# The opening of a fused Fourier-filter and maxout kernel: filter rows spread through PSUM by TensorE, X staged by ScalarE, GpSimd's pairs doubled by DMA

## The chip, the cores and the metric

One core of a Trainium2 chip runs the kernel. The metric is the device time of one execution in microseconds; it is the median of three runs. A profile is one execution recorded by the hardware profiler: its span runs from the first instruction to the last. Engines are called PE (TensorE), PEld (its weight loads), DVE (VectorE), ACT (ScalarE), POOL (GpSimd) and SP (SyncE, which here only issues DMAs).

## What is computed

The first half filters a sequence in the frequency domain; the second is a layer with two linear maps, a maximum and a third map.

```python
batch, seq, dim = (8, 3072, 256)
X = np.fft.rfft(x, axis=1)
F = (filt_r + 1j * filt_i)[None, :, :]
y = np.fft.irfft(X * F, n=x.shape[1], axis=1)      # x2 = y.reshape(24576, 256)
h1 = x2 @ w1                                       # w1, w2: 256 x 1024
h2 = x2 @ w2
out = np.maximum(h1, h2) @ w_out                   # w_out: 1024 x 256
```

## The kernel before

The transform of 3072 points is split into stages that are matrix products with small tables of sines. For a batch: stage 1 multiplies x (96 rows, 32 columns of 256) by `C1`; a transpose brings it into `bt`; stage 2 (`s2`) multiplies by the table `U` and gives the spectrum X in PSUM (`px`); a product with the filter F on a vector engine gives `pq`; stage 3 (`s3` or `s3t`) multiplies `pq` by the tables `VP` and `VQ`; a second transpose (`t2` in the first batch) gives `zr`; stage 4 (`s4`) multiplies by `G1` and gives `y_`, the filtered rows. Then `moe_h` and `moe_o` compute max(h1, h2) @ w_out as relu(x2 (w1 - w2)) @ w_out + x2 (w2 @ w_out). Eight batches are pipelined: while `moe_h` and `moe_o` run on batch b in 64 steps of eight blocks, the stages of batch b + 1 and b + 2 run between them at steps given by hand in `plan`, `mid` and `group`. The order on each engine is the order of the program (`manual_schedule`).

**The opening** is what stands ahead of the first `moe_h`: nothing of the long pipeline can cover it, so the first batch takes a shorter way, transposing through TensorE and not through DRAM (`s1t`, `t1`, `s3t`, `t2`). It runs in these steps.

- GpSimd loads x of batch 0 in eight pieces (`load_x`, L89) and F in sixteen (`load_f`, L122: two halves `WP`, columns w 0 to 8 and 8 to 12, two groups g, real and imaginary, two row blocks). Only rows 0 to 32 of each group of 64 are loaded; the other 32 rows are a copy of them, made by `double_f`: half 1 by DMAs on SP (L130), half 0 by VectorE (L128). `fix_f` (L145) then puts one row right.
- `table_c` and `tables_u` (VectorE, then sines on ScalarE, `sines_u`) make `C1` and `U`; `table_v(h, q)` turns U into the products for `VP` (q = 0) and `VQ` (q = 1) for half h of the filter pairs in PSUM, and `put_v` has ScalarE copy them. `table_g` makes `G1`.
- The twelve w columns are six pairs v = 0 to 5. For each, `s2(0, v)` gives two PSUM tiles `px`, s = 0 and 1, of 128 x 512, and each is multiplied with 1024 columns of F (real and imaginary): `product` (L390) on VectorE straight from PSUM, or on GpSimd from a copy in SBUF that ScalarE makes (`stage_x`, L652). VectorE has seven of the twelve tiles and three quarters of another (`shared_product`), GpSimd four and the remaining quarter.
- `s3t(v)` multiplies each pair's `pq` by VP and VQ: one product of `W1` that nobody reads (L581, two for v = 1), then 32 products (L587) into two PSUM tiles, which ScalarE (for g = 1 of v = 4 and 5, VectorE) evicts into `zT` (L597, L595).
- `t2(0)` transposes the first block of zT (L608), `s4(0)` makes the first `y_` (L460), and `moe_h` begins (L482). `f1` (L330 to L338) starts stage 1 of batch 1 between them.

PSUM tiles come from two pools: `ps` has six slots, `pso` two. `s3t` uses `ps` for odd v, `pso` for even; `table_v` uses `ps` for h = 0, `pso` for h = 1. A tile keeps its slot until its last reader is done. `spin(n)` issues n unread products of W1.

Pairs are done in the order 1, 0, 2, 3, 4, 5, and both halves of `table_v` and `put_v` stand ahead of the first `s3t`.

Of the kernel before, what the change touches and what calls it, by code (L numbers as in the profile page):

```python
# [27 lines left out]
def kernel(  # L28
# [29 lines left out]
    G2 = const.tile([128, 48], BF16)  # L58
    W1 = const.tile([128, 512], BF16)
# [64 lines left out]
    def double_f(h, g, ri, engine):  # L124
        w0, w1 = WP[h]
        o_, i_ = F[64 * g + 32:64 * g + 64, ri, w0:w1], F[64 * g:64 * g + 32, ri, w0:w1]
        if engine is V:
            V.tensor_copy(o_, i_)  # L128
        else:
            nc.sync.dma_start(out=o_, in_=i_)  # L130
# [13 lines left out]
    def fix_f():  # L144
        V.tensor_copy(F[32:33, 0, 0, 0], FZ[32:33, 0])  # L145
# [10 lines left out]

    hv = init.tile([128, 2, 1], FP32)
# [17 lines left out]
    for ri in range(2):  # L175
        put_fz(ri)
    load_f(0)
    load_f(1)

    def table_c():  # L180
# [10 lines left out]
        S.activation(C1, uc.rearrange("p k r -> p (k r)"), AF.Sin, bias=zero[0:NP], scale=TWO_PI)  # L191

# [58 lines left out]
    def table_g():  # L251
        pg = ps.tile([96, NP], FP32, tag="ps", name="pg")
        TE.matmul(pg, C1, I128[0:NP, 0:NP], start=True, stop=True)
# [68 lines left out]

    def f1(b, c, engine):
        if c == 0:
# [3 lines left out]
        at = at_[b]  # L328
        pa = ps.tile([96, 2, D], FP32, tag="ps", name="pa")
        TE.matmul(pa, C1, xb[b, c // 2][:, 2 * (c % 2):2 * (c % 2) + 2], start=True, stop=True)  # L330
# [9 lines left out]
    def f1_read(b):  # L340
        bt[b] = bpool.tile([128, NU, D], BF16, tag="bt", name="bt")
        src = ad[b].rearrange("(u q) m d -> (q m) u d", q=4)
        for u0, u1 in ((0, 4), (4, 12), (12, NU)):
            nc.sync.dma_start(out=bt[b][:, u0:u1], in_=src[:, u0:u1])
# [49 lines left out]
    def shared_product(v, s, px, xs_, pool):  # L394
        pq = pool.tile([128, 2, 2, D], BF16, tag="pq", name="pq")
        V.tensor_tensor(pq[:, 0], px, F[:, 0, 2 * v:2 * v + 2, s], OP.mult)
        V.tensor_tensor(pq[:, 1, 0], px[:, 0], F[:, 1, 2 * v, s], OP.mult)
        G.tensor_tensor(pq[:, 1, 1], xs_[:, 1], F[:, 1, 2 * v + 1, s], OP.mult)
        return pq
# [177 lines left out]
    def s3t(v, pq):  # L577
        pool, tag = (ps, "ps") if v % 2 else (pso, "po")
        pz = [pool.tile([128, 2, 2, 2, 2, NM], FP32, tag=tag, name="pt%d" % g) for g in range(2)]
        for _ in range(2 if v == 1 else 1):  # L580
            TE.matmul(pz[0].rearrange("p i s r c m -> p (i s r c m)"), W1[:, 0:128], W1, start=True, stop=True)  # L581
        for i in range(2):
            for s in range(2):
                for dc in range(2):
                    for q, tab in enumerate((VP, VQ)):
                        for g in range(2):
                            TE.matmul(pz[g][:, i, s, :, dc], pq[s][64 * g:64 * g + 64, q, i, 128 * dc:128 * dc + 128],  # L587
                                      tab[64 * g:64 * g + 64, 2 * v + i, s].rearrange("p (r m) -> p r m", r=2),
                                      start=(q == 0), stop=(q == 1))
        zv = zT.rearrange("p c m (w g) q -> p w g (c m) q", g=2)  # L590
        for g in range(2):
            o_ = zv[:, 2 * v:2 * v + 2, g]
            i_ = pz[g].rearrange("p i s r c m -> p i (c m) (s r)")
            if v >= 4 and g == 1:
                V.tensor_copy(o_, i_)  # L595
            else:
                S.activation(o_, i_, AF.Copy)  # L597

    def t2(c, engines):
# [3 lines left out]
        for k, engine in enumerate(engines):  # L603
            pr = ps.tile([96, n, D], BF16, tag="ps", name="pr")
            m0 = 4 * c + n * k
            for m in range(n):
                for dc in range(2):
                    TE.transpose(pr[:, m, 128 * dc:128 * dc + 128], zT[:, dc, m0 + m].rearrange("p u q -> p (u q)"),  # L608
# [14 lines left out]
    V.tensor_scalar(NI, cid, pid, -1.0, OP.is_equal, OP.mult)  # L623
    tables_u()
    for g in range(2):
        for ri in range(2):
            double_f(1, g, ri, nc.sync)
# [12 lines left out]
    zT = bpool.tile([128, 2, NM, NU, 4], BF16, tag="bt", name="zT")  # L640
    for n in range(6):
        t1(n, S if n % 2 else V)
    put_v(0, 0, table_v(0, 0))
    for g in range(2):
        for ri in range(2):
            double_f(0, g, ri, V)
    fix_f()
    xs = {}

    def stage_x(v):  # L650
        t_ = init.tile([128, 2, D], FP32, name="xs%d" % v)
        S.activation(t_, pxs[v][1], AF.Copy)  # L652
        xs[v] = t_

    POOLED = (0, 2, 3, 4)

    def products(v):
        pool = pq0 if v > 2 else pqpool
        pq = [product(V, v, 0, pxs[v][0], pool)]
        if v == 5:  # L660
            pq.append(shared_product(v, 1, pxs[v][1], xs[v], pool))
        else:
            pq.append(product(G, v, 1, xs[v], pool) if v in POOLED else product(V, v, 1, pxs[v][1], pool))
        return pq

    pqs = {}
    pxs = {v: s2(0, v) for v in (1, 0)}
    stage_x(0)
# [160 lines left out]
```

## Time and profile before

| What | Value |
|---|---|
| median of three runs | 497.84 us (497.64 to 498.34) |
| the profiled execution | 498.64 us, its span 496.8 us |
| PE busy over the span | 483.8 us (97%), 5759 products |
| DVE, ACT, POOL busy | 335.4 us (68%), 320.4 us (64%), 258.7 us (52%) |
| mean granted TensorE clock | 0.989 |
| last x piece used by `s1t` | 14.21 us |
| first product on VectorE (L390) | 23.76 us |
| first `s3t` (L581) | 25.97 us |
| `t2(0)` (L608) | 35.59 us |
| first `moe_h` product (L482) | 37.73 us |

The times in the last five rows are starts, in us from the start of the span. A busy TensorE is not TensorE at its peak, since its products are pipelined and their ends are modelled. The opening is the first 38 us, about 8% of the span; after it TensorE shows no gap longer than 1.3 us.

### The profile page before, as it was taken

How to read it: one execution, taken by the hardware profiler on the slowest of the kernel's cores; microseconds unless marked ns; L12 is line 12 of the kernel's file. 1: busy time of each engine (PE TensorE's matmuls, PEld its weight loads, DVE VectorE, ACT ScalarE, POOL GpSimd, SP SyncE). 2: the span in 40 equal slices, each digit the busy share in tenths (PEclk: the TensorE clock that was granted, in tenths of full speed). 3: DMA queues.
4: the chain of work that ended last, by engine and by line, in shares of the span. 5: the costliest groups of instructions: out<-in, count | busy, mean ns of one | idle time of the engine just before them, and what ended most of it. 6: DMA issues, size and time to landing. Idle time of an engine off the chain costs nothing.

```text
span 496.8 us, 14137 instructions
## 1 busy us (share of the span) xinstructions
PE 483.8 (97%) x5759; PEld 353.5 (71%) x5759; DVE 335.4 (68%) x535; ACT 320.4 (64%) x667; POOL 258.7 (52%) x342
## 2 busy tenths in 40 slices
PE   7699999999999999999999999999999999999997
PEld 3457777777777777777777777776777777777775
DVE  7886788468855688467855688457873688556542
ACT  5777478667775677576866668665766656464442
POOL 8694868318466594528646295536842212222220
PEclk9879999999999999999999999999999999999999
DMA  8989988996789867896789977897776834531112
GB/s 128 161 242 224 259 269 260 284 234 190 204 266 221 216 210 223 249 225 174 231 257 227 183 244 211 257 215 168 227 231 175 181 104 129 157 120 66 64 64 86
DMA packets 76626, 97.30 MB, mean 196 GB/s; under 512 B 7985, under 2 KB 54354, under 8 KB 75186
## 3 DMA queue, kind: packets, MB, share of 16 engines
q1 hardware_dynamic: 63218, 66.71, 52.1%
q0 software_dynamic: 13200, 29.60, 21.4%
q8 instruction: 45, 0.74, 0.7%
q14 instruction: 19, 0.16, 0.1%
q10 hardware_dynamic: 144, 0.09, 0.1%
HBM read 53.87 MB, written 47.19 MB: 203 GB/s over the span
## 4 chain that ended last, share of the span: by engine, by line
PE 92%; DMA 3%; ACT 2%; POOL 1%; issue 1%; DVE 0%; SPq 0%; POOLq 0%
PE po L536 34%; PE ph L482 33%; PE po L534 8%; PE pz L408 5%; PE pc L443 3%; PE px L384 2%; PE pa L355 2%; DMA xb<-in_x_dram 2%; DMA zr<-zd 1%; PE pt L587 1%; DMA zd<-zt 1%; PE pr L608 1%; POOL xb L89 1%; PE pt L581 1%; PE pa L330 1%
## 5 line engine op out<-in xcount | busy, mean ns | idle before, releaser
L486 ACT ACTIVATE gt<-ph 128x384 bf16<-128x384 f32 x357 | 175.7, 496 | 138.8 <-PE ph L482 136.2
L536 PE MATMUL po<-Wo,gt 128*128 128x256 bf16 x1528 | 262.7, 273 | 1.2 <-issue 1.2
L536 PEld LDWEIGHTS <-gt 128*128 128x128 bf16 x1528 | 144.7, 98 | 68.1 <-issue 13.5
L495 POOL DMA_DIRECT2D out_dram<-ot x186 | 103.1, 558 | 154.7 <-DVE ot L547 138.7
L390 DVE TENSOR_TENSOR pq<-px,F 128x1024 bf16<-128x1024 f32 x91 | 106.9, 1218 | 25.7 <-PE px L384 25.4
L484 DVE TENSOR_SCALAR gt<-ph 128x384 bf16<-128x384 f32 x155 | 83.6, 551 | 53.5 <-PE ph L482 47.1
L482 PEld LDWEIGHTS <-Wd 128*128 128x128 bf16 x1024 | 99.6, 98 | 13.7 <-issue 0.3
L104 POOL TENSOR_TENSOR xb<-XF 128x512 bf16<-128x512 f32 x48 | 61.3, 1277 | 66.9 <-DMA XF<-in_x_dram 31.7
L547 DVE TENSOR_SCALAR ot<-po 128x512 f32<-128x512 f32 x83 | 57.0, 686 | 35.0 <-PE po L536 33.1
L105 POOL TENSOR_TENSOR xb<-XF 128x512 bf16<-128x512 f32 x48 | 61.1, 1274 | 0.0
L359 ACT ACTIVATE at<-pa 128x512 bf16<-128x512 f32 x96 | 51.8, 611 | 3.4 <-PE pa L355 3.3
L412 ACT ACTIVATE zt<-pz 128x512 bf16<-128x512 f32 x84 | 45.6, 594 | 5.7 <-PE pz L408 1.9
L448 ACT ACTIVATE ce<-pc 128x384 f32<-128x384 f32 x56 | 23.7, 490 | 6.7 <-PE pc L443 6.0
L408 PE MATMUL pz<-pq,VP 64*64 64x256 bf16 x336 | 22.2, 281 | 0.0
L384 PE MATMUL px<-bt,U 64*64 64x256 bf16 x384 | 20.4, 283 | 1.2 <-ACT VQ L279 0.7
L408 PE MATMUL pz<-pq,VQ 64*64 64x256 bf16 x336 | 21.1, 269 | 0.0
L408 PEld LDWEIGHTS <-VP 64*64 64x64 bf16 x336 | 10.0, 105 | 13.3 <-issue 12.7
L355 PE MATMUL pa<-xb,CT 64*64 64x512 bf16 x192 | 18.0, 377 | 0.0
L443 PEld LDWEIGHTS <-zr 48*128 48x128 bf16 x896 | 13.1, 93 | 4.8 <-issue 4.4
L443 PE MATMUL pc<-G,zr 48*128 48x48 bf16 x896 | 15.4, 180 | 0.3 <-DMA zr<-zd 0.3
L384 PEld LDWEIGHTS <-U 64*64 64x64 bf16 x384 | 10.6, 109 | 3.9 <-issue 3.6
L618 PE MATMUL pd<-W 128*128 128x512 bf16 x28 | 9.2, 437 | 1.5 <-DVE zero L150 1.5
(383 smaller groups left out, 632.1 us busy)
## 6 DMA issues: line engine op xcount, KB each, us to landing
out_dram<-ot POOLq DMA_DIRECT2D x186, 128.0 KB, 3.8
XF<-in_x_dram SPq DMA_DIRECT2D x96, 192.0 KB
ad<-at SPq DMA_DIRECT2D x56, 192.0 KB
zd<-zt SPq DMA_DIRECT2D x42, 256.0 KB
zr<-zd SPq DMA_DIRECT2D x56, 192.0 KB
bt<-ad SPq DMA_DIRECT2D x13, 768.0 KB
WS<-in_moe_w_dram SPq DMA_DIRECT2D x4, 512.0 KB
xb<-in_x_dram POOLq DMA_DIRECT2D x8, 192.0 KB, 5.6
```

What stands on the lines that cost most here:

```text
L104: G.tensor_tensor(t_[:, 0], f[:, 0], f[:, 1], OP.add)
L105: G.tensor_tensor(t_[:, 1], f[:, 0], f[:, 1], OP.subtract)
L359: S.activation(at[:, m0:m0 + 2], pa[g], AF.Copy)
L390: E.tensor_tensor(pq, px.rearrange("p (o i) d -> p o i d", o=1).to_broadcast([128, 2, 2, D]), F[:, :, 2 * v:2 * v + 2, s], OP.mult)
L408: TE.matmul(pz[g][64 * s:64 * s + 64, i], tab[64 * g:64 * g + 64, 2 * v + i, s], pq[s][64 * g:64 * g + 64, q, i], start=(q == 0), stop=(q ...
L412: S.activation(zt[:, :, g], pz[g], AF.Copy)
L482: TE.matmul(ph, Wd[:, dc, 128 * j:128 * j + 128], y_[:, dc], start=(dc == 0), stop=(dc == 1))
L484: V.tensor_scalar(gt[tt][:, j], ph, 0.0, None, OP.max)
L486: S.activation(gt[tt][:, j], ph, AF.Relu)
L495: E.dma_start(out=dst, in_=ot[tt // 2][:, 3 * (tt % 2) + c])
L536: TE.matmul(p_, g_[:, n - 2, blk], Wo[:, n - 2], start=(e == 0), stop=(e == 9))
L547: V.tensor_scalar(ot[tt // 2][:, e - 1:e + 1], po[q // 2 % 2], SCALE, None, OP.mult)
```

## The change

It rewrites the opening and moves some work of the first batch's steps.

- **F.** VectorE no longer doubles half 0. SP doubles columns w 6 to 8 and 8 to 12, both real and imaginary in one DMA, so pairs 3, 4 and 5 are whole. For pairs 0, 1 and 2 TensorE multiplies the 32 loaded rows by `E2`, a doubled identity, into a PSUM tile `sp` (`spread`): the doubled filter, 512 columns at a time. `E0` and a saved row `NQ` do what `fix_f` did. VectorE doubles w 0 to 6 later, in four copies at steps 13, 15, 17 and 19, and GpSimd fixes the row at step 20, for the later batches.
- **Products.** ScalarE stages both halves of X for pairs 0 to 4 in SBUF. VectorE multiplies `sp` with the staged X, two half products (real, imaginary) for each of the six tiles of pairs 0 to 2. GpSimd takes both tiles of pair 3, one of pair 4 and half of the other; VectorE the other half and both tiles of pair 5, these from PSUM.
- **Order.** Pairs go 1, 2, 0, 3, 5, 4 through `s3t`. `table_v` always uses `pso`; `s3t` uses `ps` for 2, 3 and 4, `pso` for 1, 0 and 5. `put_v(0,0)` stands ahead of `t1`, the other three between the `s3t`. Five of six `t1` evictions are VectorE's. `busy(n)` puts n unread products (tile `pf`, which keeps a slot of `ps`) at nine places, `fill(n)` four more (a slot of `pso`) after the setup.
- **zT** gets a layout with the block of four m outermost; the columns of G1 are permuted to suit (`CP`). The eviction of the last pair is cut in two, the first eighth first, which is all that `t2(0)` reads.
- **f1** is split into `f1_in` (TensorE) and `f1_out` (eviction and DMA); four `f1_in` stand before the first `moe_h`, the evictions after `s4(0)` or at steps 1 and 2. `f1_read` becomes three planned pieces. Loads and folds of batch 2 move by 1 to 4 steps; loads of batch 1 and `prep_wd` are reordered on GpSimd.

The diff, cut:

```diff
...
+    def double_f(w0, w1, g):
+        nc.sync.dma_start(out=F[64 * g + 32:64 * g + 64, :, w0:w1], in_=F[64 * g:64 * g + 32, :, w0:w1])
+
+    def put_nq():
+        G.tensor_copy(NQ[32:33], FZ[32:33, 0])
+
+    def double_v(w0, w1, g, ri):
+        V.tensor_copy(F[64 * g + 32:64 * g + 64, ri, w0:w1], F[64 * g:64 * g + 32, ri, w0:w1])
...
-        V.tensor_copy(F[32:33, 0, 0, 0], FZ[32:33, 0])
+        G.tensor_copy(F[32:33, 0, 0, 0], NQ[32:33])
...
+    put_nq()
+    fix_f()
...
+        S.activation(CP.rearrange("p (g w c) -> p g w c", g=2, c=4),
+                     uc.rearrange("p (w g s) r -> p g w (s r)", g=2, s=2), AF.Sin, bias=zero[0:NP], scale=TWO_PI)
...
-        pool, tag = (pso, "po") if h else (ps, "ps")
-        pv = [pool.tile([128, 6, 64], FP32, tag=tag, name="pv%d" % s) for s in range(2)]
+        pv = [pso.tile([128, 6, 64], FP32, tag="po", name="pv%d" % s) for s in range(2)]
...
+    def f1_in(b, c):
+        pas[c] = ps.tile([96, 2, D], FP32, tag="ps", name="pa")
+        TE.matmul(pas[c], C1, xb[b, c // 2][:, 2 * (c % 2):2 * (c % 2) + 2], start=True, stop=True)
...
+    def table_e():
+        for g in range(2):
+            for c in range(2):
+                S.activation(E2[64 * g:64 * g + 32, 32 * c:32 * c + 32], I128[64 * g:64 * g + 32, 64 * g:64 * g + 32],
+                             AF.Copy)
+        for c in range(2):
+            S.activation(E0[0:33, 32 * c:32 * c + 32], I128[0:33, 0:32], AF.Copy)
+        S.activation(E0[0:33, 32:33], I128[0:33, 32:33], AF.Copy)
+
+    def spread(v, s, ri):
+        sp = ps.tile([128, 2, D], FP32, tag="ps", name="sp")
+        for g in range(2):
+            r = slice(64 * g, 64 * g + 32)
+            if g == 0 and (v, s, ri) == (0, 0, 0):
+                TE.matmul(sp[0:64, 0], E0[0:33], F[0:33, 0, 0, 0], start=True, stop=True)
+                TE.matmul(sp[0:64, 1], E2[r], F[r, 0, 1, 0], start=True, stop=True)
+            else:
+                TE.matmul(sp[64 * g:64 * g + 64], E2[r], F[r, ri, 2 * v:2 * v + 2, s], start=True, stop=True)
+        return sp
...
-        pool, tag = (ps, "ps") if v % 2 else (pso, "po")
-        pz = [pool.tile([128, 2, 2, 2, 2, NM], FP32, tag=tag, name="pt%d" % g) for g in range(2)]
-        for _ in range(2 if v == 1 else 1):
-            TE.matmul(pz[0].rearrange("p i s r c m -> p (i s r c m)"), W1[:, 0:128], W1, start=True, stop=True)
+        pool, tag = (ps, "ps") if v in (2, 3, 4) else (pso, "po")
+        pz = [pool.tile([128, 8, 2, 2, 2, 2, 4], FP32, tag=tag, name="pt%d" % g) for g in range(2)]
+        TE.matmul(pz[0].rearrange("p o i s r c m -> p (o i s r c m)"), W1[:, 0:128], W1, start=True, stop=True)
...
+                            TE.matmul(pz[g][:, :, i, s, :, dc].rearrange("p o r m -> p r o m"),
+                                      pq[s][64 * g:64 * g + 64, q, i, 128 * dc:128 * dc + 128],
+                                      tab[64 * g:64 * g + 64, 2 * v + i, s].rearrange("p (r o m) -> p r o m", r=2, m=4),
                                       start=(q == 0), stop=(q == 1))
...
+        for o0, o1 in ((0, 1), (1, 8)) if v == 4 else ((0, 8),):
+            for g in range(2):
+                o_ = zT[:, o0:o1, :, :, g, 2 * v:2 * v + 2].rearrange("p o c m w q -> p o (c m) (w q)")
+                i_ = pz[g][:, o0:o1].rearrange("p o i s r c m -> p o (c m) (i s r)")
+                if v > 3 and g == 1:
+                    V.tensor_copy(o_, i_)
+                else:
+                    S.activation(o_, i_, AF.Copy)
...
+    table_e()
...
+    for w0, w1 in ((6, 8), (8, 12)):
+        for g in range(2):
+            double_f(w0, w1, g)
...
+    zT = bpool.tile([128, 8, 2, 4, 2, NW, 4], BF16, tag="bt", name="zT")
     put_v(0, 0, table_v(0, 0))
...
+    def stage_x(v, s):
+        xs[v, s] = init.tile([128, 2, D], FP32, name="xs%d%d" % (v, s))
+        S.activation(xs[v, s], pxs[v][s], AF.Copy)
+
+    def spread_product(v, s, n=0):
+        pq = pq_pool(v).tile([128, 2, 2, D], BF16, tag="pq", name="pq")
         for ri in range(2):
+            if ri:
+                busy(n)
+            V.tensor_tensor(pq[:, ri], spread(v, s, ri), xs[v, s], OP.mult)
+        pqs[v].append(pq)
+
+    def pooled_product(v, s):
+        pqs[v].append(product(G, v, s, xs[v, s], pq_pool(v)))
+
+    def shared_product(v, s):
+        pq = pq_pool(v).tile([128, 2, 2, D], BF16, tag="pq", name="pq")
+        for ri, E in enumerate((V, G)):
+            E.tensor_tensor(pq[:, ri], xs[v, s], F[:, ri, 2 * v:2 * v + 2, s], OP.mult)
+        pqs[v].append(pq)
+
+    def plain_product(v, s):
+        pqs[v].append(product(V, v, s, pxs[v][s], pq_pool(v)))
+
+    for n in (1, 0, 2, 3, 5, 4):
+        t1(n, V if n else S)
+    pf = ps.tile([128, 512], FP32, tag="ps", name="pf")
+
+    def busy(n):
+        for _ in range(n):
+            TE.matmul(pf, W1[:, 0:128], W1, start=True, stop=True)
+
+    pxs[1] = s2(0, 1)
+    for s in range(2):
+        stage_x(1, s)
+    sines_u(1)
+    busy(2)
+    spread_product(1, 0, 4)
+    pxs[2] = s2(0, 2)
+    stage_x(2, 0)
+    pxs[3] = s2(0, 3)
+    for s in range(2):
+        stage_x(3, s)
+    spread_product(1, 1)
+    stage_x(2, 1)
+    spread_product(2, 0)
+    for s in range(2):
+        pooled_product(3, s)
+        load_x(1, 2 * s, 2)
     put_v(0, 1, table_v(0, 1))
-    pxs[2] = s2(0, 2)
-    stage_x(2)
-    sines_u(1)
+    busy(2)
+    spread_product(2, 1)
+    pxs[0] = s2(0, 0)
+    for s in range(2):
+        stage_x(0, s)
+    s3t(1, pqs[1])
+    spread_product(0, 0, 1)
+    pxs[4] = s2(0, 4)
+    for s in range(2):
+        stage_x(4, s)
+    pooled_product(4, 0)
+    busy(1)
+    s3t(2, pqs[2])
+    spread_product(0, 1, 1)
+    pxs[5] = s2(0, 5)
     put_v(1, 0, table_v(1, 0))
-    pxs[3] = s2(0, 3)
-    stage_x(3)
+    busy(4)
+    s3t(0, pqs[0])
+    plain_product(5, 0)
+    shared_product(4, 1)
     put_v(1, 1, table_v(1, 1))
-    for v in (1, 0, 2):
-        pqs[v] = products(v)
-        if v == 0:
-            load_x(1, 0, 2)
-    s3t(1, pqs[1])
-    pxs[4] = s2(0, 4)
-    stage_x(4)
-    pqs[3] = products(3)
-    s3t(0, pqs[0])
-    pxs[5] = s2(0, 5)
-    stage_x(5)
-    for v in (2, 3):
+    busy(2)
+    s3t(3, pqs[3])
+    plain_product(5, 1)
+    busy(3)
+    for v in (5, 4):
         s3t(v, pqs[v])
-    for v in (4, 5):
-        pqs[v] = products(v)
-    for v in (4, 5):
-        s3t(v, pqs[v])
-    load_x(1, 2, 2)
...
+    prep_wd(0, G)
+    load_x(1, 4, 2)
+    prep_wd(1, G)
     load_wo()
-    prep_wd(0, G)
-    for c in (4, 6):
-        load_x(1, c, 2)
-    for q in range(1, 4):
-        prep_wd(q, G)
+    prep_wd(2, G)
+    load_x(1, 6, 2)
+    prep_wd(3, G)
...
+    f1_in(1, 0)
+    fill(1)
     t2(0, (V, S))
-    f1(1, 1, V)
-    spin(1)
+    f1_in(1, 1)
+    f1_in(1, 2)
+    fill(1)
     s4(0)
-    f1(1, 2, S)
-    f1(1, 3, V)
+    f1_in(1, 3)
+    f1_out(1, 0, S)
+    f1_out(1, 1, V)
+    fill(2)
...
     plan(0, 1, t2, 1, (V,))
+    plan(0, 1, f1_out, 1, 2, S)
+    plan(0, 2, f1_out, 1, 3, V)
...
+    for n, (g, ri) in zip((13, 15, 17, 19), ((0, 0), (0, 1), (1, 0), (1, 1))):
+        plan(0, n, double_v, 0, 6, g, ri)
+    plan(0, 20, fix_f)
...
     plan_f2(0, (25, 28, 31, 35, 38, 42, 46), ((0,), (), (1,), (2,), (3,), (4,), (5, 6)),
-            (8, 8, 10, 12, 17, 20, 24, 28), (10, 13, 16, 20, 24, 27, 30, 33))
+            (8, 8, 12, 14, 17, 21, 24, 27), (10, 13, 20, 23, 26, 29, 32, 36))
...
```

More of the change, by code (lines that the diff above doesn't have):

```diff
@@ L710, with fill @@
     gpool = ctx.enter_context(tc.tile_pool(name="gpool", bufs=2))
-    f1(1, 0, S)
-    spin(1)
+    pd = pso.tile([128, 512], FP32, tag="po", name="pd")
+    def fill(n):
+        for _ in range(n):
+            TE.matmul(pd, W1[:, 0:128], W1, start=True, stop=True)
+    f1_in(1, 0)
+    fill(1)
     t2(0, (V, S))
-    f1(1, 1, V)
-    spin(1)
+    f1_in(1, 1)
+    f1_in(1, 2)
+    fill(1)
     s4(0)
-    f1(1, 2, S)
-    f1(1, 3, V)
+    f1_in(1, 3)
+    f1_out(1, 0, S)
+    f1_out(1, 1, V)
+    fill(2)
     todo = {}
@@ L728, in plan_f1 @@
             plan(b, n, f1, nb, c, S if c % 2 == 0 else V)
-        plan(b, read, f1_read, nb)
+        for k, (u0, u1) in enumerate(((0, 4), (4, 12), (12, NU))):
+            plan(b, read + k, f1_read, nb, u0, u1)
     mid = {}
```

77 lines of the change are left out of this document (19 added, 58 removed).

## The prediction

> **What bounds the kernel now.** I read the page, then the windows of the opening, then the timelines of VectorE, ScalarE, GpSimd and TensorE between 14 and 40 us, then the chain of waits over the same stretch. The chain says that TensorE holds the span, and the windows say from when:
>
> ```profile
> PE 92%; DMA 3%; ACT 2%; POOL 1%; issue 1%; DVE 0%; SPq 0%; POOLq 0%
> ...
> 15.00:20.00 5.00, 4.14 (x90) 3.51 (x91) 3.91 (x6) 3.66 (x7) 3.72 (x8) 1.00 1.24 170
> 20.00:25.00 5.00, 2.51 (x88) 1.44 (x88) 4.75 (x6) 3.78 (x9) 3.80 (x3) 0.63 0.69 129
> 25.00:30.00 5.00, 4.79 (x127) 2.75 (x126) 5.00 (x5) 3.33 (x8) 4.99 (x4) 0.50 0.75 204
> ```
>
> Each window gives start:end, length, then busy time of PE, PEld, DVE, ACT and POOL with counts, PE clock, DMA share, GB/s. Between 20 and 30 us VectorE is full (4.75 and 5.00 of 5), TensorE is half idle at first and its clock falls to 0.50. From the first `moe_h` product at 37.73 us TensorE waits for almost nothing (two waits, 1.5 us in all), so the change is worth what it moves that point by, nearly one for one. The point hangs on `t2(0)`, at 35.59. The engines before it:
>
> ```profile
> 18.49 4.76 DVE L128 COPY F<-F 32x4096 bf16<-32x4096 bf16 x4
> 23.28 0.28 DVE L145 CAST F<-XF 1x256 bf16<-1x256 f32 x1
> 23.76 8.13 DVE L390 TENSOR_TENSOR pq<-px,F 128x1024 bf16<-128x1024 f32 x7 [0.19 <-DVE F L145]
> 31.80 0.68 DVE L396 TENSOR_TENSOR pq<-px,F 128x512 bf16<-128x512 f32 x1
> ...
> 16.43 2.85 ACT L573 ACTIVATE bt<-pb 128x1024 bf16<-128x1024 bf16 x3 [1.34 <-PE pb L570]
> 22.47 0.60 ACT L652 ACTIVATE xs<-px 128x512 f32<-128x512 f32 x1 [0.37 <-PE px L384]
> 22.97 0.93 ACT L249 ACTIVATE U<-ua,zero 128x768 bf16<-128x768 f32 x1
> 24.52 0.87 ACT L279 ACTIVATE VP<-pv 128x384 bf16<-128x384 f32 x2 [0.63 <-PE pv L265]
> 32.03 3.28 ACT L597 ACTIVATE zT<-pt 128x512 bf16<-128x512 f32 x6 [0.37 <-PE pt L587]
> ...
> 19.82 2.40 POOL L122 DMA_DIRECT2D F<-in_filt_i_dram  x2
> 23.43 2.12 POOL L390 TENSOR_TENSOR pq<-xs,F 128x1024 bf16<-128x1024 f32 x1 [1.20 <-DVE F L128]
> ```
>
> A row is start, duration, engine, line, what it writes and reads. VectorE's copies (L128) keep its products back until 23.76; it then runs to 32.8. The chain of waits shows a second limit, the two slots of pool `pso`:
>
> ```profile
> 29.08 1.01 PE pt L587 x30
> 30.10 0.59 ACT zT L597
> 30.69 0.04 issue
> 30.73 0.59 PE pt L581
> ```
>
> `s3t(2)` starts 0.04 us after ScalarE empties a tile of `s3t(0)`.
>
> **VectorE's share.** Removed: 4.76 + 0.28 us of copies, and 4 of 7 full products at a pitch of (8.13 - 1.22)/6 = 1.15. Added: 12 half products; the nearest row is L396, 0.68 long at a pitch of 0.60, so 7.2 us (bounds 0.60 and 1.15 each; the shape is L396's, so 0.60). It keeps two full products and a half (2.9) and takes two more evictions of `t1`. Its products can start at 19.55 in place of 23.76: the last `t1` eviction now ends at 19.36, and `px` of pair 1 is staged at 19.45. With the waits below it is done by about 32.3. So VectorE no longer sets the end, but it was not alone in setting it.
>
> **Filter load.** Two small casts on GpSimd (0.28 to 0.54 each, by L145 and L142) come ahead of the loads of F. POOL's 17th issue (15.28) and its 21st (18.11) each wait for a filter load to land; read as eight out at a time, the 13th landed at 18.1, and SP's first doubling (20.79) shows the 17th: a pace of 0.68, so the 16th, which the second `spread` needs, lands at 20.1 (to 20.6 with the casts). Held back by up to 1 us, F leaves the DMA engines to the last x pieces for longer (they land about 1 us apart, the last at 14.2): 0 to 0.5 earlier for all that follows, I take 0.2. At the other end, POOL's last two issues take 2.40 us for two beside VectorE's copies, 0.49 to 0.58 each elsewhere; without the copies about 1.3 us is won there. [...]
>
> **GpSimd and the DMA doubling.** SP now doubles 768 KB, not 512 (256 KB more, about 1.3 us at the mean 196 GB/s). GpSimd has three full products at 2.12, one half at 1.06 and two load issues at 0.55: 8.5 us. The doubling of pair 3 is issued at about 20.7; landing 3.3 to 6.7 later, as F's loads do (the answer on tile F; 24.0 to 27.4), GpSimd ends at 32.5 to 35.9. `s3t(4)`'s products need it at 35.9 below: covered, at the far end just so, and a later landing would cost its whole lateness.
>
> **ScalarE is the new ledger.** At 512 columns a row is 0.60 long at a pitch of 0.49 (22.47 to 22.97). `table_e` and CP are eight small operations (0.23 to 0.38 each) ahead of L225, up to 1 us, covered by ScalarE's later idle of 0.74 and 0.44 us; I add 0.1. `put_v(0,0)` moves to the gap at 15.1 and two `t1` evictions leave, but ten stagings replace five. TensorE ends `t1` at 18.2, `px` of pair 1 is there at 18.85. ScalarE, in program order, then has before `put_v(1,0)`: ten stagings 4.9, the sines 0.83, `put_v(0,1)` 1.0, four evictions 1.96; 8.69 us, so 27.54 at best. Waits between, from rows: `px` of pair 2 is behind the spread that waits for F (20.25; 0.27 lost), `table_v(0,1)` is behind four spreads that take slots as stagings and products free them (0.56), `s2(0,0)` behind the fill and two spreads (0.30), `s2(0,5)` and `table_v(1,0)` behind `s3t(2)` and two spreads (0.48). A spread is unseen: two 512-column products cost 0.43 in a row by the fill's pitch 0.215, 0.22 side by side as `s2`'s eight are (0.24 at 61.75). I take 0.30; ends -0.5 and +0.8 on this point. That gives 29.15 for `put_v(1,0)`.
>
> **From there a chain that nothing hides.** `table_v(1,x)`, `s3t(0)` and `s3t(5)` share the two `pso` slots, in order on TensorE, and ScalarE empties them:
>
> - `put_v(1,0)`, 0.87: 30.02
> - `s3t(0)`, 0.05 + 0.70 (34.05 to 34.76 for `s3t(5)` now): 30.77
> - its two evictions, 0.49 + 0.60: 31.86
> - `table_v(1,1)`, 0.05 + 0.65 (20.33 to 20.98 now): 32.55
> - `put_v(1,1)`, 0.87: 33.42; only now can `s3t(3)` run, as it reads those tables
> - `s3t(3)`'s 32 products, 0.05 + 0.58: 34.05
> - `busy(3)`, 3 x 0.215: 34.70 (its cover would be a late product; VectorE ends at 32.3, so it has none)
> - `s3t(5)`, 0.32 + 0.58: 35.60
> - `s3t(4)`, 0.32 + 0.70: 36.62
> - eviction of its first eighth, 64 columns, 0.25 + 0.13: `t2(0)` at 37.0.
>
> Before, `table_v(1,1)` was done at 26.0, ahead of every `s3t`, and `s3t` ran at 0.90 each; the new order puts three of them behind it. So `t2(0)` moves from 35.59 to 37.0, +1.4, although the cut eviction saves 0.4 (0.69 before). The strided `s3t` output and eviction are unseen; I cost them as now (at worst +0.4 each, as at half clock).
>
> **After `t2(0)`.** `f1_out` leaves the path: VectorE's `y_` need not wait for L333 (-0.15). Four pending `pa` hold slots in exchange; their fills lie in waits. At steps 13 to 19 VectorE gets 4 copies of 3072 columns, 0.9 each by L128's 1.22 for 4096: 3.6 us into 50 to 58 us, where it is busy 6.5 of 8, so about 2 us late, with 1.4 idle at 58 to catch up before its product at 62.2. Queued behind a copy are evictions of `ph`, for which TensorE waits when six slots are full: 0 to 1, I take 0.2. The split `f1_read` and later folds keep their slack; nothing.
>
> Sum: 0.1 - 0.2 + 1.4 - 0.15 + 0.2 = +1.35. Against the profiled 498.64 us (span 496.8, 1.84 around it) that is 500.0; that execution lies 0.80 above the median 497.84, so **499.2**.
>
> **Rivals.** (a) ScalarE never waits before `put_v(1,0)`: 1.6 earlier, `t2(0)` at 35.4, total 497.6: no change. For it: the waits I find are each under 0.6 us, no more than the error of the spreads; against: four engines feed each other in one fixed order. (b) Faster: the slot wait is not real at `table_v(1,1)`. Then ScalarE's row of work decides: 18.85 + 8.69 + 1.6 + 0.83 + evictions of 0, 3 and 5 (2.45) + `put_v(1,1)` 0.83 + 0.25 = 33.5, `t2(0)` at 33.9, -1.7, total 496.1 with the other terms. It decides once `table_v(1,1)` starts before 30. For it: VectorE is freed by 3 us; against: the row at 30.73. (c) The clock falls again. Now it fell after three us with PE busy 0.32, 0.41 and 0.05 of 1; a half-clock `s3t` (28.48 to 30.05) costs 0.6 more than a full one; four of them and the fills make +3, total 502. [...] (d) The copies only move and stall TensorE at steps 13 to 20 for their full overflow: 2 more, total 501.2.
>
> **Chances.** A measurement of this kernel tells 0.2%, 1.0 us, from no change. Forecast 0.43, own range 498.2 to 500.7; of it 0.31 is over +1.0. (a) 0.19, within. (b) 0.27, faster. (c) 0.06 and (d) 0.05, slower. So slower 0.42, same 0.31, faster 0.27. The range runs from 496.1, which leaves half of (b) out, to 501.6, which leaves (c) out: 0.195 outside.
>
> **What would show it.** Right: no L128 in the opening, PE clock near 1.00 from 20 to 30, `s3t(3)` starting right after a `put_v` past 33 us, `t2(0)` near 37. Wrong: `table_v(1,1)` before 31, then (b); products of VectorE or GpSimd ending after 34, then the fill had cover; clock 0.50, then (c); VectorE late by more than two steps at 50 to 60, then (d).

## The result, and the profile after

The changed kernel takes 501.65 us (median of 4 runs, 501.44 to 502.29) against 498.09 us (497.64 to 498.72) for the kernel before in the same comparison: 1.0073 times as long, with a 95% interval of 1.0055 to 1.0090. The forecast was 499.2 with a range of 496.1 to 501.6. The direction was right, the size was not: +3.6 us in place of +1.35. The profiled execution took 502.29 us with a span of 500.5, 3.7 more than the span of before (496.8). Of the variants below, some unprofiled executions have a mean granted clock of 0.98 to 0.997 in place of 1.000 and are some 1 to 6.5 us longer, for a reason that no trace here shows, so parts of the time are read from the profiled executions, with the median and its range beside them.

First the shares of the chain of waits, then the windows of the opening of the changed kernel (start:end, length; busy time of PE, PEld, DVE, ACT and POOL with counts; TensorE clock, DMA share, GB/s):

```profile
PE 89%; DMA 6%; POOL 2%; DVE 1%; SPq 1%; issue 0%; POOLq 0%
...
20.00:25.00 5.00, 4.55 (x83) 1.75 (x80) 3.48 (x6) 3.39 (x8) 1.22 (x2) 1.00 0.68 142
25.00:30.00 5.00, 5.00 (x96) 2.25 (x94) 3.05 (x5) 4.37 (x9) 4.98 (x5) 1.00 0.79 236
30.00:35.00 5.00, 4.01 (x126) 2.35 (x125) 5.00 (x4) 3.04 (x7) 4.99 (x5) 1.00 1.08 254
```

VectorE is no longer full from 20 to 30 us (3.48 and 3.05 of 5) and the clock stays at 1.00, both as the change meant it. ScalarE's timeline, with the idle time ahead of each row and its releaser in brackets:

```profile
18.64 1.08 ACT L680 ACTIVATE xs<-px 128x512 f32<-128x512 f32 x2 [1.11 <-PE px L400]
19.61 0.94 ACT L258 ACTIVATE U<-ua,zero 128x768 bf16<-128x768 f32 x1
21.60 2.06 ACT L680 ACTIVATE xs<-px 128x512 f32<-128x512 f32 x4 [1.05 <-PE px L400]
24.23 0.40 ACT L286 ACTIVATE VQ<-pv,zero,hv 128x64 bf16<-128x64 f32 x1 [0.56 <-PE pv L277]
24.53 0.81 ACT L287 ACTIVATE VQ<-pv 128x320 bf16<-128x320 f32 x2
25.57 1.09 ACT L680 ACTIVATE xs<-px 128x512 f32<-128x512 f32 x2 [0.23 <-PE px L400]
26.55 1.09 ACT L626 ACTIVATE zT<-pt 128x512 bf16<-128x512 f32 x2
28.02 1.09 ACT L680 ACTIVATE xs<-px 128x512 f32<-128x512 f32 x2 [0.38 <-PE px L400]
29.12 1.09 ACT L626 ACTIVATE zT<-pt 128x512 bf16<-128x512 f32 x2
30.71 0.87 ACT L287 ACTIVATE VP<-pv 128x384 bf16<-128x384 f32 x2 [0.50 <-PE pv L273]
32.40 1.09 ACT L626 ACTIVATE zT<-pt 128x512 bf16<-128x512 f32 x2 [0.81 <-PE pt L615]
34.12 0.87 ACT L287 ACTIVATE VQ<-pv 128x384 bf16<-128x384 f32 x2 [0.64 <-PE pv L277]
35.85 1.08 ACT L626 ACTIVATE zT<-pt 128x512 bf16<-128x512 f32 x2 [0.85 <-PE pt L615]
37.41 0.60 ACT L626 ACTIVATE zT<-pt 128x512 bf16<-128x512 f32 x1 [0.47 <-PE pt L615]
38.30 0.66 ACT L626 ACTIVATE zT<-pt 128x64 bf16<-128x64 f32 x2 [0.30 <-PE pt L615]
```

From `put_v(1,0)` (30.71) down, ScalarE and TensorE take turns, and each row waits for the one before it: the chain through the two slots of `pso` that the prediction wrote out. It ends in `t2(0)` at 38.71 in place of 35.59. Of this, 0.3 us is a wait of TensorE inside `s3t(3)` for nothing that the profile shows; the second profile (e11) and those of e4 to e6 do not have it.

```profile
35.24 0.21 PE L615 MATMUL pt<-VP,pq 64*128 64x64 bf16 x2 [0.27 <-issue]
```

What comes later was read by the lag: for each of the 64 blocks, when its first `moe_h` product starts, less the start of the same one before. Each trace has its own accidents, so both kernels were profiled a second time (the last column but one; the runs are in the next section).

| part | 1st profiles, after less before | 2nd profiles | predicted |
|---|---|---|---|
| first `moe_h` product (block 0) | 40.93 - 37.73 = +3.20 | 40.78 - 38.23 = +2.55 | +1.15 |
| wait for `Wd`, blocks 0 to 2 | +0.74 | +0.05 | none |
| copies of F, blocks 2 to 4 | +1.54 | +1.40 | +0.2 |
| blocks 4 to 39 | +0.03 | +0.23 | none |
| blocks 39 to 41 (321 to 337 us) | -1.83 | -1.21 | none |
| end (span) | +3.7 | +3.0 | +1.35 |

### The profile page after: what moved, and what is told of

It is laid out like the page before. It is cut to its first block, busy times and chain, and to the rows that moved or that the text cites. A ratio compares the mean times of both kernels' runs of the same rounds, so it can differ in the third digit from the quotient of the medians.

```text
span 500.5 us, 14256 instructions
## 1 busy us (share of the span) xinstructions
PE 490.9 (98%) x5805; PEld 355.3 (71%) x5805; DVE 340.2 (68%) x543; ACT 323.4 (65%) x679; POOL 257.8 (51%) x344
## 3 DMA queue, kind: packets, MB, share of 16 engines
q0 software_dynamic: 13200, 29.60, 21.2%
## 4 chain that ended last, share of the span: by engine, by line
PE 89%; DMA 6%; POOL 2%; DVE 1%; SPq 1%; issue 0%; POOLq 0%
PE po L565 34%; PE ph L511 33%; PE po L563 8%; PE pz L437 5%; DMA WS<-in_moe_w_dram 3%; PE pc L472 3%; PE pa L371 2%; PE px L400 2%; DMA F<-in_filt_i_dram 2%; DMA xb<-in_x_dram 2%; POOL xb L92 1%; DVE F L134 1%; POOL Wd L306 1%; PE pa L339 0%; PE pr L637 0%; DVE gt L513 0%
## 5 line engine op out<-in xcount | busy, mean ns | idle before, releaser
L406 DVE TENSOR_TENSOR pq<-px,F 128x1024 bf16<-128x1024 f32 x86 | 101.3, 1219 | 25.4 <-PE px L400 25.4
L437 PE MATMUL pz<-pq,VQ 64*64 64x256 bf16 x336 | 21.2, 269 | 0.0
L400 PE MATMUL px<-bt,U 64*64 64x256 bf16 x384 | 19.1, 272 | 0.0
```

Of the source, the lines that this page charges most:

```text
L406: E.tensor_tensor(pq, px.rearrange("p (o i) d -> p o i d", o=1).to_broadcast([128, 2, 2, D]), F[:, :, 2 * v:2 * v + 2, s], OP.mult)
L437: TE.matmul(pz[g][64 * s:64 * s + 64, i], tab[64 * g:64 * g + 64, 2 * v + i, s], pq[s][64 * g:64 * g + 64, q, i], start=(q == 0), stop=(q ...
```

## The experiments

In the diffs, a line of "..." leaves code out. "t2(0)" is its start in the profiled execution (38.71 in the first profile after), "lag" is against the first profile of before.

**The tables of V ahead of the chain** (e1). `put_v(1,x)` no longer stands between the `s3t`.

```
+    put_v(0, 1, table_v(0, 1))
     sines_u(1)
...
-    put_v(0, 1, table_v(0, 1))
+    put_v(1, 0, table_v(1, 0))
     busy(2)
...
+    put_v(1, 1, table_v(1, 1))
     s3t(1, pqs[1])
...
-    put_v(1, 0, table_v(1, 0))
     busy(4)
...
-    put_v(1, 1, table_v(1, 1))
     busy(2)
```

> The changed kernel with the three later tables taken out from between the s3t: put_v(0,1) ahead of the second sines, put_v(1,0) where put_v(0,1) stood, put_v(1,1) ahead of s3t(1). In the changed kernel t2(0) starts at 38.71 us, 3.12 after the kernel before. Slot chain (table_v(1,1) behind the evictions of s3t(0) sets the end): the chain is gone, but VectorE's last product of pair 5 ends at 36.23 behind a half product of 3.23 us, so s3t(5) waits for it: t2(0) at 38.2 to 38.5, about 0.3 us less in all (501.3). If the chain alone counts and VectorE's long product gives way too: t2(0) at 36.3, 499.2. TensorE's sum (fills and spreads fill it, the order does not matter): t2(0) stays at 38.7.

Measured: 502.23 us (502.01 to 502.40), t2(0) 38.56: nothing won. The chain after `s3t(0)`'s eviction got shorter, 34.38 to 38.56 = 4.2 us in place of 38.71 - 32.40 = 6.3, but it starts 2.0 later. TensorE's row and VectorE's show why:

```profile
27.59 0.38 PE L609 MATMUL pt<-W 128*128 128x512 bf16 x1 [1.08 <-ACT VQ L287]
...
24.41 2.48 DVE L687 TENSOR_TENSOR pq<-sp,xs 128x512 bf16<-128x512 f32 x4
29.26 1.29 DVE L687 TENSOR_TENSOR pq<-sp,xs 128x512 bf16<-128x512 f32 x2 [2.38 <-ACT zT L626]
```

`s3t(1)` now waits 1.08 us until `put_v(1,1)` has freed the two slots of `pso`. The spread for pair 0 stands behind it in TensorE's order, starts at 28.53 in place of 26.36 and ends at 29.16, and VectorE, which reads it, idles 2.38 us until then. The bracket names an eviction that ends at about the same time; in the changed kernel, too, this product starts 0.1 us after its spread.

**VectorE's half of the shared product with one SBUF input** (e2), and both edits together (e3).

```
-        for ri, E in enumerate((V, G)):
-            E.tensor_tensor(pq[:, ri], xs[v, s], F[:, ri, 2 * v:2 * v + 2, s], OP.mult)
+        V.tensor_tensor(pq[:, 0], spread(v, s, 0), xs[v, s], OP.mult)
+        G.tensor_tensor(pq[:, 1], xs[v, s], F[:, 1, 2 * v:2 * v + 2, s], OP.mult)
```

> The changed kernel with VectorE's half of the shared product taking the filter from PSUM (one more spread) and not from SBUF, so that it has one SBUF input and not two. Both theories expect that product to fall from 3.23 to about 0.69 us, if it was held by GpSimd working on SBUF at the same time. Slot chain: the end does not hang on it, t2(0) stays at 38.6 to 38.9 and the time at 501.7. Blocked VectorE (its late last product sets the end): t2(0) up to 2.4 us earlier, 36.3, and 499.3 in all. If contention is not the cause, the product stays near 3 us.

> Both edits together. Slot chain with the blocked product as the next limit behind it: t2(0) at 36.2 to 36.8, the time 499.3 to 499.8, far more than the two edits alone add up to. Two independent causes: the sum of the two. TensorE's sum: 38.7, 501.7.

The reason for these is one row of VectorE's timeline of the changed kernel, and below it GpSimd's beside it:

```profile
31.87 3.23 DVE L696 TENSOR_TENSOR pq<-xs,F 128x512 bf16<-128x512 f32 x1
...
31.71 1.16 POOL L696 TENSOR_TENSOR pq<-xs,F 128x512 bf16<-128x512 f32 x1
32.83 1.27 POOL L306 TENSOR_TENSOR Wd<-WS 128x512 bf16<-128x512 f32 x1
34.60 1.61 POOL L306 TENSOR_TENSOR Wd<-WS 128x512 bf16<-128x512 f32 x1
```

The half product reads both operands from SBUF and ends only at 35.10, after GpSimd's two instructions without a gap; the same size with one operand in PSUM takes 0.69. Measured in e2: 0.69 for the new row, but 502.49 us (501.69 to 503.18) and t2(0) 38.84. So the 2.5 us that VectorE won end in a wait: its last product has cover, for `s3t(5)` comes behind `s3t(3)` and `busy(3)` in TensorE's order anyway. The trace of e2 alone does not settle this, since TensorE stands 0.85 us inside `s3t(3)` there, for a `put_v(1,1)` that had ended 0.8 us before; what it waited for is not shown. Four other traces settle it, in which the opening's products are those of the changed kernel. The two-input product took 0.73 in e4, 0.68 in e6, 1.58 in e5 and 1.65 in e11, and from `put_v(1,0)` to `t2(0)` all four need 7.70 or 7.71 us. In e3: 502.45 us (501.92 to 503.65), t2(0) 39.44; the 2.38 us idle is there again (at 29.82). Miss for the theory that these two are what makes the opening late.

**The copies of F in the steady stage**: by two transfers of SP in place of VectorE (e4), or by VectorE but at steps 8, 9, 9, 10 (e5).

```
-    for n, (g, ri) in zip((13, 15, 17, 19), ((0, 0), (0, 1), (1, 0), (1, 1))):
-        plan(0, n, double_v, 0, 6, g, ri)
+    for g in range(2):
+        plan(0, 3 + g, double_f, 0, 6, g)
```

> The changed kernel with the four later VectorE copies of F (steps 13 to 19) replaced by two DMAs on SP at steps 3 and 4. In the changed kernel the lag behind the kernel before grows from 3.94 us at moe block 2 to 5.48 at block 4. If VectorE's copies do that: the lag stays at 3.9 to 4.1, the time 1.4 to 1.5 less, 500.2. Rival (what stalls there is the later fold or the split read of bt, or the DMAs' 768 KB now delay XF and bt): the lag still grows by 1 or more, 501.2 or above.

> The changed kernel with VectorE's four later copies of F at steps 8, 9, 9 and 10 in place of 13, 15, 17 and 19, where VectorE was idle (2.06 us before 51.70) and GpSimd too (46.7 to 53.6). If the copies' place sets what the lag gains between moe blocks 2 and 4 (1.54 us): at most 0.4 is left of it, the time about 1.2 less than the changed kernel. If the later folds or the split read of bt do it: 1.3 or more stays.

Measured: e4 500.01 us where profiled, 504.40 in the median (500.01 to 505.95); e5 501.13 where profiled, 503.73 (501.13 to 504.77). In both traces the lag stays level up to block 4 (2.44 to 2.54, and 2.31 to 2.43), where the changed kernel adds 1.54: that sum is the copies'. By the medians neither edit gains anything (501.65 without them), and between blocks 4 and 5 a part comes back, 0.59 and 1.58 us. ScalarE of e5 there:

```profile
80.85 1.08 ACT L441 ACTIVATE zt<-pz 128x512 bf16<-128x512 f32 x2 [1.78 <-DMA zd<-zt]
```

It waits for a transfer to free `zt`, and TensorE waits 1.42 us for it. Time won ahead of that transfer is partly lost at it.

**Three of the four loads of x(1) behind the first quarters of `Wd`** (e6), so that the weights land first.

```
         pooled_product(3, s)
-        load_x(1, 2 * s, 2)
+        if s == 0:
+            load_x(1, 0, 2)
...
     prep_wd(0, G)
-    load_x(1, 4, 2)
-    prep_wd(1, G)
     load_wo()
+    prep_wd(1, G)
+    load_x(1, 2, 2)
     prep_wd(2, G)
-    load_x(1, 6, 2)
+    load_x(1, 4, 2)
     prep_wd(3, G)
+    load_x(1, 6, 2)
```

> The changed kernel with three of the four loads of batch 1's x moved behind the first two quarters of Wd on GpSimd's queue, so that fewer bytes compete with the moe weights. If those loads hold the weights back (the third quarter of Wd waits for them until 41.47): that wait goes from 4.37 us to under 1, the lag between moe blocks 0 and 1 grows by 0.1 and not 0.73, 0.6 less in all. If the weights are late for another reason (SP issues them behind the doubling DMAs): the wait stays over 3 us and the lag grows by 0.6 or more.

Measured: 502.52 us (501.87 to 505.68). The third `prep_wd` starts at 37.72 in place of 41.47 without a wait, but the lag grows by 1.30 between blocks 0 and 1. The waits from 43 to 44.2 us (line waited for: us, times, longest) name the new one:

```profile
PEld L339 <- DMA xb<-in_x_dram: 1.4, 1, 1.4
```

The last piece of x(1) is late now, 1.4 us, where in the first profile of the changed kernel the third `prep_wd` waited 4.37 us for the weights. Here moving the loads of x(1) changed which of the two is waited for.

**The tables in ScalarE's idle times** (e8): `put_v(0,1)` among the `t1`, `put_v(1,0)` in place of the fill inside the first spread, `put_v(1,1)` where `put_v(0,1)` was; and the same with the one-input product (e9).

```
-    for n in (1, 0, 2, 3, 5, 4):
+    for n in (1, 0, 2):
         t1(n, V if n else S)
+    put_v(0, 1, table_v(0, 1))
+    for n in (3, 5, 4):
+        t1(n, V)
...
-            if ri:
+            if ri and (v, s) == (1, 0):
+                put_v(1, 0, table_v(1, 0))
+            elif ri:
                 busy(n)
...
-    put_v(0, 1, table_v(0, 1))
+    put_v(1, 1, table_v(1, 1))
     busy(2)
```

> The changed kernel with the three later tables put where ScalarE stood idle: put_v(0,1) between the transposes of t1 (idle 17.5 to 18.6), put_v(1,0) in place of the fill before the second spread (idle 20.5 to 21.6), put_v(1,1) where put_v(0,1) stood (24.2). Unlike in e1, no table then stands ahead of a spread that VectorE waits for. Slot chain: the tables leave the path from 29.7 on; then VectorE's blocked half product (3.23 us) is next, t2(0) at 38.0 to 38.4, 0.5 less. VectorE's pace or TensorE's sum as the cause of the late end: t2(0) at 38.5 to 38.9.

> e8 with VectorE's half of the shared product taken from PSUM, one SBUF input. Slot chain, with the blocked product behind it: t2(0) at 36.0 to 36.6, the first moe_h at 38.4 to 38.8, the time about 2.3 less than the changed kernel, 499.3. TensorE's sum: not before 38.

Measured: e8 501.23 us where profiled, 502.71 in the median (500.49 to 507.72), t2(0) 37.81; e9 501.04 and 501.34 (500.16 to 506.38), t2(0) 37.29, the earliest of all. The two starts cannot be compared as they stand, for the last piece of x landed at 14.89 in e8 and at 14.04 in e9. From that landing to `t2(0)` e4, e5 and e6 take 23.73 us each, e8 22.92, e9 (and e12 below) 23.25. So the tables in ScalarE's idle times win 0.8 us, and the one-input product costs 0.3 of it: its extra spread stands in TensorE's order ahead of `s3t(3)`, whose eviction waits 0.57 for TensorE in e9 and 0.24 in e8, and in e8 the two-input product took 0.68 anyway. With no table left between the `s3t`, ScalarE of e9 idles instead:

```profile
29.70 1.09 ACT L626 ACTIVATE zT<-pt 128x512 bf16<-128x512 f32 x2
32.79 1.08 ACT L626 ACTIVATE zT<-pt 128x512 bf16<-128x512 f32 x2 [2.00 <-PE pt L615]
```

There `s3t(0)` waits for VectorE, whose last spread product (30.11 to 31.40) itself waited 1.16 us for a spread that TensorE's order puts behind `s3t(2)`. So the slot chain is a bound, but another lies 0.5 to 0.8 us under it (23.25 and 22.92 us from the landing, against 23.73).

**Both kernels once more** (e10 is the kernel before, e11 the changed one, without an edit).

> The kernel before, unchanged, profiled a second time. In the first profile TensorE lost 0.28 us at 325.98 to a transfer and 1.23 us at 336.35 in an idle time that nothing explains, and every trace of a changed kernel is 1.8 us less far behind after that stretch. Theory: these stalls belong to the kernel before (its transfers and instruction stream at that place), so they come again, and the changed kernels gain 1.8 us there whatever their opening does. Rival: they were an accident of one execution; then the second profile lacks them, its span is about 495.0 in place of 496.8, and the 1.8 us are no part of the change. t2(0) again at 35.6 within 0.3, the granted clock at 0.50 from 22 to 30.

> The changed kernel, unchanged, profiled a second time. Kernels with the same opening started t2(0) at 37.8 (the copies at other steps, the loads of x moved, the copies by DMA) and at 38.7 (the first profile): if this is the landing of the filter in that execution, t2(0) now comes between 37.7 and 38.9 with the second spread's product of VectorE between 20.6 and 21.3, each later by the same amount; VectorE's half of the shared product takes 3.2 us where GpSimd's queue has no gap beside it and under 1.6 where GpSimd waits for the expert's weights; the third prep_wd starts between 38 and 41.5. The rival, that t2(0) is always at 38.7 in this kernel: then it is not the landing. The copies at steps 13 to 19 cost TensorE 1.2 to 1.6 us between blocks 2 and 4 either way.

Measured: e10 498.37 us, span 496.6, t2(0) 36.09; e11 501.39 us, span 499.6, t2(0) 38.56. The kernel before is 0.50 us later at block 0 than in its first profile and has no wait at 325.98, but the other stall comes again; TensorE's rows of its first and second profile:

```profile
325.98 0.77 PE L443 MATMUL pc<-G,zr 48*128 48x48 bf16 x47 [0.28 <-DMA zr<-zd]
336.35 0.28 PE L536 MATMUL po<-Wo,gt 128*128 128x256 bf16 x1 [1.23 <-issue]
...
336.11 0.28 PE L536 MATMUL po<-Wo,gt 128*128 128x256 bf16 x1 [1.04 <-issue]
```

So some 1.0 to 1.2 us at 336 us are in both profiles of the kernel before, and in no profile of the changed kernel or its variants; what TensorE waits for there, neither profile shows. The wait at 325.98, 0.45 us by the lag, was an accident. In the changed kernel the copies cost 1.40 again; the weights' wait is gone (0.05), and with GpSimd's queue open (a wait of 1.74 us for the weights) VectorE's two-input product takes 1.65. The second spread waits for the filter here too:

```profile
20.96 0.40 PE L427 MATMUL sp<-F,E 32*64 32x512 bf16 x1 [0.71 <-DMA F<-in_filt_i_dram]
```

**The edits of e9 and e4 in one** (e12).

> All that helped, in one: tables put in ScalarE's idle times, VectorE's half of the shared product with one SBUF input, and the copies of F in the steady stage done by SP's transfers in place of VectorE. Theory: t2(0) 37.3 as with the first two, the lag behind the kernel before 1.8 at the first moe_h, 2.5 after the weights' wait, no growth at steps 13 to 19, about 3.1 at block 5 and 1.3 at the end: 499.2 to 500.0 where the clock stays at 1.0. So even with the parts mended the opening is not shorter than before's. Rival: the parts are coupled and the copies' 1.5 us come back as waits for transfers of the steady stage: then 501 and more, as with the copies by DMA alone in its other executions.

Measured: 501.26 us where profiled, 504.70 in the median (501.26 to 507.01). Up to block 4 it holds, t2(0) 37.51 and a lag of 2.00 to 2.11; then ScalarE waits 1.97 us for the transfer of `zt`, and block 5 is at 3.88. The rival was right: with the copies gone their time comes back as that wait. No version beats the kernel before.

**Without a fill** (e13). `busy(n)` issues nothing; the fills, 20 products by the trace (the expectation counts 27), are left out.

```
     def busy(n):
-        for _ in range(n):
+        for _ in range(0):
```

> The changed kernel without any busy fill (27 products of 128x512 whose result nobody reads are left out). Theory: the fills are what holds the granted clock at 1.00 between 20 and 40 us; without them TensorE is busy under half of the time from 20 to 34, the clock falls to 0.50, the s3t's take about 1.0 us in place of 0.6 and the spreads twice as long; against that stand the 9 fills behind put_v(1,0) that lie on the chain (9 x 0.215 = 1.9 us, of which busy(4) lies beside a wait). t2(0) between 38.5 and 41, the whole 502 to 504.5. Rival: the clock does not fall, or the fills cost as much as they save; then t2(0) 37 to 38 and 500 to 501.5.

Measured: 502.84 us (502.03 to 503.33), t2(0) 39.95. Its windows:

```profile
25.00:30.00 5.00, 5.00 (x76) 2.15 (x74) 1.71 (x4) 3.34 (x7) 4.98 (x5) 0.50 0.95 299
30.00:35.00 5.00, 3.48 (x114) 2.40 (x114) 5.00 (x4) 2.27 (x6) 4.99 (x6) 0.50 1.02 249
```

The clock falls to 0.50 and stays there to 35 us (0.54 in the mean from 35 to 40); with the fills it is 1.00 in each of these windows, in both profiles. The filter was in time here as in e4 to e6. Against those, `put_v(1,0)` starts at 30.90 in place of 30.06 to 30.24, and from there to `t2(0)` it takes 9.05 us in place of 7.71. So in these runs the fills hold the clock at 1.00; they are worth 2.0 us up to `t2(0)` (25.78 us from the landing of x in place of 23.73) and 1.2 us by the medians of the whole.

## Why the prediction missed

**Right in kind: VectorE's share, the chain, the clock.** VectorE's spread products took 0.69 and a pitch of 0.64 (3.87 for six) where 0.60 was put; no copy is left in the opening; rival (c), the clock, did not come (1.00 from 20 to 35 us), and e13 shows that the fills are why (0.50 from 25 to 35 us without them). GpSimd's last product ends at 32.87, inside the 32.5 to 35.9 put. "From there a chain that nothing hides" held: from `put_v(1,0)` to `t2(0)` 37.0 - 29.15 = 7.85 us predicted, 8.00 measured in the first profile (0.3 of it the wait inside `s3t(3)`) and 7.70 in the second, with every row in the order written. Rival (b), that the slot wait is not real at `table_v(1,1)`, is out: `put_v(1,1)` starts at 34.12, after `s3t(0)`'s evictions. Products did end after 34 (VectorE's last at 36.23), which was to mean cover for the fill; it did, but the cover decides nothing, as the chain has the same length in e4 and e6, where VectorE ends at 33.27 and 33.04.

The reading behind rival (c) was off. The granted clock of before is 1.00 up to 21.2 us and 0.50 from 21.4 on, so the three us with PE busy 0.32, 0.41 and 0.05 (21 to 24, clock 0.64, 0.50 and 0.50) lie but for their first 0.2 to 0.4 us behind the fall, not ahead of it. In the three us ahead of it (18.2 to 21.2) TensorE was busy 0.66; in e13 the clock fell at about 22.5 (an estimate from its mean of 0.75 between 20 and 25), behind three us at 0.74; the changed kernel kept 1.00 through three us at 0.68 (31.0 to 34.0). So these busy shares do not tell when the clock falls.

**The first step that failed: "waits between" in "ScalarE is the new ledger".** The row of work was right, the waits were put at 1.6 us and measured 2.72 (the five brackets of the timeline between 19.61 and 30.71), with another 0.65 that a sum by pitches leaves out: a row that nothing follows takes its full 0.60, not the pitch of 0.49, and five waits make five such rows, 0.55. So `put_v(1,0)` starts at 30.71, not 29.15. In the five traces with this opening (e4, e5, e6 and the two profiles) it starts at 30.06 to 30.86, all later than 29.95, which is the 29.15 with the 0.8 that the prediction allowed for the unseen spreads. By name: `table_v(0,1)` 0.56 as put, `s2(0,0)` 0.23 (0.30 put), `table_v(1,0)` 0.50 (0.48 put). Mis-sized was `px` of pair 2, 1.05 in place of 0.27, and a wait for `s2(0,4)` was not in the sum at all, 0.38.

The wait for `px` of pair 2 has two parts. In e4, e5 and e6 the filter was in time and the wait is still 0.61, and all five together 2.30; the spread stands behind the four fills there (19.37 to 20.4 in e4), and in e13, without fills, this wait is gone. The rest is the filter's landing, the step **"Filter load"**: what the second `spread` needs was to land at 20.1. In the chain of waits of the changed kernel it lands at 20.77. First the row that issues it, before and after, then the chain:

```profile
14.45 0.57 POOL L122 DMA_DIRECT2D F<-in_filt_i_dram  x1 [0.87 <-DMA xb<-in_x_dram]
...
14.53 0.57 POOL L125 DMA_DIRECT2D F<-in_filt_i_dram  x1 [0.92 <-DMA xb<-in_x_dram]
...
14.53 6.24 DMA F<-in_filt_i_dram
20.77 0.28 issue
```

The load is issued as early as before; both times the issue waits for a piece of x. What varies from one execution to the next is the time to landing: 6.24 and 6.90 us in the two profiles of the changed kernel, 4.82 to 5.66 in e4, e5 and e6, which do not touch these loads and have it landed by 19.32 to 20.03. So 20.1 was a fair figure, and both profiles of the changed kernel fell on the late side of it. Counted from the landing of the last piece of x, which itself comes between 13.73 and 14.25 in these five traces, `t2(0)` comes 23.73 us later in e4, e5 and e6. It is 24.46 in the first profile (0.44 more of wait for the filter, 0.29 for the wait inside `s3t(3)`) and 24.83 in the second (1.10 more for the filter). With the filter in time `t2(0)` is at 37.77 to 37.95 and still 0.8 to 0.95 past the forecast of 37.0. That is what the step itself was short: 0.7 of waits and 0.65 of broken pitches, less the earlier start of x (`stage(1,0)` at 18.43 to 18.61 for 18.85) and a chain shorter by 0.14.

After `t2(0)` the prediction took 0.15 off for `f1_out`. From `t2(0)` to the first `moe_h` product it is 2.14 us in both profiles of before and 2.22 in both of the changed kernel, so this gain did not come.

**The second: "I take 0.2" for the copies in "After t2(0)".** It measured 1.54 and 1.40, shown by e4 and e5, which have none of it there. Rival (d) had put 2 on this and got a chance of 0.05. Duration was right for a copy alone (0.95 for 0.9 put). What failed was the catching up: the 1.4 us of idle time at 58 to 60 lie behind the `y_` of that block in VectorE's queue, and the four copies were put ahead of it. VectorE's rows of before, then those of the changed kernel and TensorE's wait:

```profile
57.80 0.56 DVE L466 TENSOR_SCALAR y__1335<-py 128x384 bf16<-128x384 f32 x1 [0.22 <-PE py L460]
59.77 0.69 DVE L611 COPY zr<-pr 96x1024 bf16<-96x1024 bf16 x1 [1.41 <-PE pr L608]
...
56.36 1.74 DVE L134 COPY F<-F 32x3072 bf16<-32x3072 bf16 x1
58.13 1.02 DVE L513 TENSOR_SCALAR gt<-ph 128x384 bf16<-128x384 f32 x2
...
63.52 0.95 DVE L134 COPY F<-F 32x3072 bf16<-32x3072 bf16 x1
64.51 0.56 DVE L513 TENSOR_SCALAR gt<-ph 128x384 bf16<-128x384 f32 x1
64.98 0.55 DVE L495 TENSOR_SCALAR y__1420<-py 128x384 bf16<-128x384 f32 x1
...
65.58 0.32 PE L511 MATMUL ph<-y__1420,Wd 128*128 128x384 bf16 x1 [0.86 <-DVE y__1420 L495]
```

The same `y_` is at 57.80 before; with the lag of 3.93 it would be at 61.73, so VectorE is 3.25 us late when it is asked, and idle time that follows is of no use to it. The evictions of `ph`, which the prediction watched, were not the victim.

**Not in the prediction at all.** The wait for `Wd`, +0.74 in one profile and +0.05 in the other: SP issues the weights' loads when its doublings are through, from 25.1 on in both first profiles, and in the profile with the wait the last, issued at 27.36, takes 13.97 us to land. That the loads of x(1) compete with it is only argued, from e6, where the order decides which is late. And the stall at 336 us, absent from every profile with the change: 1.2 us of gain that nobody could read out of the diff, and whose link to the change is not shown.

**The sum** from the second profiles: 2.55 + 0.05 + 1.40 + 0.23 - 1.21 = 3.0, the difference of the spans. The forecast's 1.35 lacks 1.4 in the opening and 1.2 in the copies. The gain at 336 us hides part of both, which was luck; without it the miss would have been larger.

**Still open:** what the stall at 336 us and the waits inside `s3t(3)` wait for; why the filter's landing varies by 1.6 us (19.32 to 20.91) between the five traces; and what bounds the opening of e8, e9 and e12, which is still later than before's.

## What to carry to other kernels

When work leaves the full engine for three others, sum each of the others as a row with its interruptions: here five waits of ScalarE cost their 2.72 us and 0.55 more in broken pitches. Idle time pays for added work only where it stands ahead of what is waited for in that engine's queue; here 1.4 us of idle time stood behind the `y_`, and the copies cost 1.54 and 1.40. Look for the next consumer behind the insertion, not for the free share of the window. And two bounds less than 1 us apart hide each other: after one was taken out, the end moved by little (0.8 us in e8, 0.5 in e9), so a part's worth cannot be read from one removal. Before two traces are compared, take out what differs from one execution to the next, here the landing of the last input: t2(0) made e9 look 0.5 us better than e8, and from the landing it is 0.3 worse.

## What the runs showed of the hardware

VectorE's product of 128x512 with both inputs in SBUF took 0.68 us where GpSimd had ended or was about to (e1, e6, e8), 1.58 and 1.65 where it started beside the one GpSimd product (e5, e11), and 3.23 beside two GpSimd instructions without a gap. It ended 0.57 after GpSimd's product in e5 and e11. In the row of 3.23 it started 0.16 after GpSimd's product; GpSimd's next instruction started at 32.83 and took 1.27 all the same, and VectorE ended 1.00 after that. GpSimd's product took 1.15 or 1.16 each time (e1, e5, e11, the first profile after). In e1 VectorE came first, and GpSimd's `prep_wd`, from 0.04 us later on, took 1.78 in place of 1.27. With one input in PSUM, VectorE's product took 0.69 in e12, though it started at 33.44 beside a `prep_wd` of 1.27 that ran from 32.70. That VectorE waits for GpSimd when both its inputs are in SBUF is the author's estimate from these lengths; how it comes about is not shown.

The copies in the steady stage are longer beside GpSimd too: the first, beside a fold, takes 1.60 and 1.74 us, the others 0.95, and the fold that follows 1.98 and 2.00 in place of 1.27. That fold starts 0.87 and 0.85 us before the copy's end. So VectorE may have come in between two folds without a gap here, an estimate from these lengths.

The half clock of e13 lengthens the chain from `put_v(1,0)` to `t2(0)` by 1.3 us (9.05 against the 7.71 of e4 to e6), its own fills being left out. The 3 us that the prediction put on rival (c) counted slowed fills as well, so the two are not the same case.
